# Taking the products of no use out of the first steps of a one-core attention and FFN kernel

## The chip, the cores and the metric

The kernel runs on one core of one Trainium2 chip. The metric is the device time of one execution in microseconds (us). Five engines take part, each with its own queue in order: TensorE (PE, with its weight loads as PEld), VectorE (DVE), ScalarE (ACT), GpSimd (POOL) and SyncE (SP, which issues most of the DMAs here).

## The reference

Eight batches of eight heads, 576 tokens each of head size 64. A packed query `p` of 32 rows attends over `k` and `v`, and then the 576 queries attend over the 32 packed rows, as keys and as values. The result is laid out as 4608 tokens of 512 features and goes through a two-layer FFN with a leaky activation.

```python
def sm_attn(qq, kk, vv):
    s = scale * np.matmul(qq, kk.transpose(0, 1, 3, 2))
    a = np.exp(s - np.max(s, axis=-1, keepdims=True))
    a = a / (np.sum(a, axis=-1, keepdims=True) + 1e-09)
    return np.matmul(a, vv)
p_packed = sm_attn(p, k, v)
out = sm_attn(q, p_packed, p_packed)          # -> x, 4608 x 512
h = x @ w_in                                  # 512 x 2048, float64
g = np.maximum(h, 0.0) + alpha * np.minimum(h, 0.0)
y = g @ w_out                                 # 2048 x 512, float64
```

The two weights come in as float64, and the kernel turns them into float32 by operations on their bits.

## The kernel before, in words

Heads lie in four pairs, and an FFN block is a block of 128 of the 2048 inner features. The kernel never forms x: it multiplies the packed values of a batch into `w_in` (`packed_w`, tile `pw`) and then the attention weights into that (`first`, tile `ps_h`). So an FFN block of half a batch (a "tile" k, 288 tokens) is `first(k, f)`, an activation on ACT (L783, `neg`) and one on DVE (L797, `g`), and `second(k, f)`, which adds into the four banks `acc`. In the first blocks of batch 0 these products are in plain float32 (L770 for `first`, L892 for `second`); later they are in three float32r products each (L776 to L778, and L895 to L897 or L828).

**The first steps.** Before the blocks begin, the prologue `go("...")` walks through a string, one letter for each step: `a` and `b` take one step of the attention of batch 0 and of batch 1; `i` and `o` load a piece of `w_in` or `w_out`, and `I`, `O`, `A` convert one; `0` multiplies packed values into a piece of `w_in`; `n` loads alpha. The steps of batch 0 on TensorE are in this order: the scores of `p` with `k` (L376 into `acc` from `praw`), transposes of the softmax (L653, one row of heads after the other), the products with `v` (L670), a transpose of the packed values (L513), the scores of `q` with them (L376 into `acc` from `p`), and the product into `w_in` (L376 into `ps_m` from `w`). Then the loop over blocks begins: the first piece of `pieces` is "aabb", so the scores of batch 1 (L376 into `ps_m` from `xraw`) come among the first L770 and L892.

**The products of no use.** The letters `u`, `v`, `w`, `x` call `keep_busy`, which multiplies an identity by itself into a bank that nothing reads. `v` and `w` begin with one product (L280) that reads a result of DVE (the row maxima `m0`, the row sums `z0`), so that the rest (L284) start no earlier than that.

```python
    def keep_busy(n, behind_value):
        spare = ps_h.tile([P, 512], F32, name="spare", tag="h")
        with ExitStack() as behind:
            behind.enter_context(tc.issue_after(last_mm[0].ins))
            if behind_value is not None:
                nc.tensor.matmul(
                    spare[:, : behind_value.shape[-1]], ident, behind_value, start=True, stop=True
                )
            for _ in range(n):
                last_mm[:] = [nc.tensor.matmul(spare[:, :P], ident, ident, start=True, stop=True)]
    BUSY = {"u": 7, "v": 4, "w": 4, "x": 3, "y": 3, "z": 2}
    BEHIND = {"v": "m0", "w": "z0", "z": "m1"}
```

`last_mm` is read by `keep_busy` alone. The bank `spare` has the tag `h`, of which there are two; the tiles `ps_h` of the blocks and one tile of transposes (`ps_j`) use the same two.

**What sets the order.** Each engine works off its own queue in the order that was written when the program was built. The program is built with `schedule_with_timeline_sim=True`: a planner chooses among instructions by their place in the code and by a timeline that it reckons, except where `issue_after` fixes an instruction behind another one on its engine. From place 41 of the loop on, and around the joints before that, TensorE's order is fixed by `last_pe`.

Of the kernel before, what the change touches and what calls it, by code (L numbers as in the profile page):

```python
# [27 lines left out]
def pack_attention_ffn_kernel(  # L28
# [153 lines left out]
    def load(out, in_):  # L182

        with ExitStack() as behind:
            if queue:
                behind.enter_context(tc.issue_after(queue[-1].ins))
            ins = nc.sync.dma_start(out=out, in_=in_)  # L187
        if written:
            queue[:] = [ins]
# [84 lines left out]
# [11 lines that stand above are left out]
# [414 lines left out]
    def packed_w(b, j, parts=(None,), tag=None):  # L699

        banks = [bank(tag) for _ in range(2)]
        for part_ in parts:
            to = slice(0, 512) if part_ is None else slice(part_ * 256, part_ * 256 + 256)
            for pr, r, rs, cs in heads():
                w = wi_t[j, pr] if part_ is None else w0[part_][:, pr]
                in_turn(b, banks[r][cs, to], p2[b][rs, cs], w[rs, :])
        to = slice(0, 512) if len(parts) == 2 or parts[0] is None else to
        if in_f32(b, 4 * j):
            if j % 2 == 0 and parts[0] in (None, 0):
                two_pw[:] = [pwp.tile([P, 2, 2, 512], F32, name="pw", tag="pw")]  # L710
            here = two_pw[0][:, j % 2]
        elif (b, j) == (B - 1, NJ - 1):
            here = vin.tile([P, 2, 2, 512], F32R, name="pw", tag="vraw", bufs=1)
        else:
            here = pwp.tile([P, 2, 2, 512], F32R, name="pw", tag="pw")
        times = 2.0 if half_in(j) else 1.0
        for r in range(2):
            ps = banks[r][:, to]
            if in_f32(b, 4 * j):
                a = nc.scalar.activation(out=here[:, r, to], in_=ps, func=AF.Copy, scale=times)  # L720
                anchor(b, a)
                if not first_pw and r:
                    first_pw.append(a)
            else:
                hi, lo = here[:, 0, r, to], here[:, 1, r, to]
                nc.scalar.activation(out=hi, in_=ps, func=AF.Copy, scale=times)  # L726
                nc.vector.scalar_tensor_tensor(
                    out=lo, in0=ps, scalar=times, in1=fv(hi), op0=ALU.mult, op1=ALU.subtract
                )
        for n in range(to.start // P, to.stop // P):  # L730
            cs = slice(n * P, n * P + P)
            pw[b, 4 * j + n] = here[:, :, cs] if in_f32(b, 4 * j) else here[:, :, :, cs]
# [218 lines left out]
    def go(what):  # L951


        for ch in what:
            if ch in BUSY:
                keep_busy(BUSY[ch], values[BEHIND[ch]] if ch in BEHIND else None)
            elif ch == "n":
                load(al, alpha)
                nc.gpsimd.tensor_scalar(
                    out=nal, in0=al, scalar1=-1.0, scalar2=1.0, op0=ALU.mult, op1=ALU.add  # L960
                )
            elif ch in "ab":
                next(a0 if ch == "a" else a1, None)
            elif ch in counts:
                n = counts[ch]
                counts[ch] += 1
                if ch == "0":
                    if n < 2:
                        packed_w(0, 0, (n,))
                    else:  # L970
                        packed_w(0, n - 1)
                elif ch == "1":
                    packed_w(1, n, (None,) if n else (0, 1))
                else:
                    with ExitStack() as behind:
                        for ins in tail.values() if ch != "A" else []:
                            behind.enter_context(tc.issue_after(ins.ins))
                        {
                            "i": w_in_load, "I": w_in_convert, "o": w_out_load,
                            "O": w_out_convert, "S": w_out_late_split, "H": late_a, "A": w_out_begin,  # L980
                        }[ch](n)

    go("ainaaauoiaaaIaboaiiaa0abooavbxawaOI")
    tail.clear()
    written.clear()

# [134 lines left out]
```

## Time and profile before

| what | value |
|---|---|
| median of 3 runs | 714.98 us (714.53 to 716.31) |
| the profiled execution's own time | 716.52 us |
| its span in the trace | 714.7 us |
| PE busy | 700.0 us, 98% of the span |
| DVE busy | 474.6 us, 66% |
| ACT busy | 358.2 us, 50% |
| mean granted TensorE clock | 0.993 |

The span runs from the first to the last instruction in the trace; 1.8 us of the execution's own time lie outside it. The granted clock is the share of TensorE's full speed that the throttle let through; 1.00 stands for 2.4 GHz and 0.50 for 1.2 GHz. Busy times of PE are modelled at their ends, so that the busy spans of two products in a row overlap by the tail of the first. A float32 product shows as two records.

### The profile page before, as it was taken

To read this page: it belongs to the slowest core of one execution; us is meant where nothing else is said; L and a number is where in the kernel's file an instruction comes from. 1 tells how busy PE (TensorE), PEld (TensorE's weight loads), DVE (VectorE), ACT (ScalarE), POOL (GpSimd) and SP (SyncE) were. 2 spreads that over 40 slices of the span, in tenths; PEclk is the share of its full clock that TensorE was granted. 3 is DMA by queue.
4 is the path that set the end of the run, shared out by engine and by line. 5 is a ranking of instruction groups with operands and counts; after the bars stand their busy time and mean duration, and the time that the engine had idled before them with its cause. 6 is when DMAs were issued, how large, how long until landed. Compare 5 with 4: busy or idle time off the path is not lost.

```text
span 714.7 us, 14609 instructions
## 1 busy us (share of the span) xinstructions
PE 700.0 (98%) x5604; PEld 600.7 (84%) x5604; DVE 474.6 (66%) x1067; ACT 358.2 (50%) x846; POOL 32.8 (5%) x128
## 2 busy tenths in 40 slices
PE   6999999999999999999999999999999999999997
PEld 3666998999998888888878888888887888798897
DVE  3899897974696559656783567846694446964443
ACT  3787688854355544545453454545352333533232
POOL 1000200002001100001000010001000000000000
PEclk9799999999999999999999999999999999999999
DMA  8996464332544413442314523325214103010100
GB/s 262 382 335 243 148 218 168 118 104 80 157 154 152 129 39 126 148 150 78 126 28 136 145 77 126 118 75 148 81 76 148 51 25 95 24 30 1 30 16 30
DMA packets 76740, 85.36 MB, mean 119 GB/s; under 512 B 34944, under 2 KB 56960, under 8 KB 76672
## 3 DMA queue, kind: packets, MB, share of 16 engines
q1 hardware_dynamic: 76448, 84.25, 36.6%
q8 instruction: 44, 0.72, 0.4%
q14 instruction: 24, 0.20, 0.1%
q10 hardware_dynamic: 224, 0.20, 0.1%
HBM read 70.79 MB, written 13.63 MB: 118 GB/s over the span
## 4 chain that ended last, share of the span: by engine, by line
PE 91%; DVE 4%; ACT 2%; DMA 1%; SPq 1%; issue 0%; ACTq 0%; DVEq 0%
PE acc L828 40%; PE ps_h L776 9%; PE ps_h L778 9%; PE ps_h L777 9%; PE acc L895 5%; PE acc L896 5%; PE acc L897 5%; PE ps_m L376 4%; PE ps_j L376 3%; PE acc L892 2%; PE acc L376 2%; DMA vtwo<-in_v 1%; SPq L187 1%; PE ps_h L770 1%; PE acc L928 0%
## 5 line engine op out<-in xcount | busy, mean ns | idle before, releaser
L828 PE MATMUL acc<-wo,gh 128*128 128x512 f32 x704 | 200.1, 398 | 0.0
L783 ACT ACTIVATE neg<-ps_h 128x256 f32<-128x256 f32 (+2 forms) x256 | 105.0, 411 | 161.4 <-PE ps_h L778 153.9
L797 DVE SCALAR_TENSOR_TENSOR neg<-neg,nal,ps_h 128x256 f32<-128x256 f32 (+1 forms) x248 | 119.7, 484 | 76.1 <-ACT neg L783 75.6
L807 ACT CAST gh<-neg 128x256 fp32r<-128x256 f32 (+1 forms) x248 | 101.8, 411 | 113.5 <-DVE neg L797 112.3
L776 PE MATMUL ps_h<-a_h,pw 128*128 128x256 f32 (+2 forms) x496 | 146.4, 295 | 0.4 <-DVE neg L797 0.4
L778 PE MATMUL ps_h<-a_h,pw 128*128 128x256 f32 (+2 forms) x496 | 146.6, 296 | 0.0
L777 PE MATMUL ps_h<-a_l,pw 128*128 128x256 f32 (+2 forms) x496 | 146.5, 295 | 0.0
L808 DVE TENSOR_TENSOR gl<-neg,gh 128x256 fp32r<-128x256 f32 (+1 forms) x248 | 104.7, 426 | 61.6 <-ACT gh L807 59.8
L828 PEld LDWEIGHTS acc<-wo,gh 128*128 128x128 f32 x704 | 126.7, 195 | 21.9 <-issue 4.2
L828 PE MATMUL acc<-wo,gl 128*128 128x512 f32 x352 | 115.5, 394 | 0.0
L776 PEld LDWEIGHTS ps_h<-a_h,pw 128*128 128x128 f32 x496 | 93.4, 188 | 7.4 <-DVE neg L797 1.1
L777 PEld LDWEIGHTS ps_h<-a_l,pw 128*128 128x128 f32 x496 | 93.4, 188 | 7.2
L778 PEld LDWEIGHTS ps_h<-a_h,pw 128*128 128x128 f32 x496 | 93.5, 189 | 0.1
L896 PE MATMUL acc<-gh,wo 128*128 128x288 f32 (+1 forms) x280 | 79.7, 293 | 0.5 <-DVE wo L235 0.5
L828 PEld LDWEIGHTS acc<-wo,gl 128*128 128x128 f32 x352 | 68.6, 195 | 13.5
L895 PE MATMUL acc<-gh,wo 128*128 128x288 f32 (+1 forms) x280 | 79.8, 296 | 0.0
L897 PE MATMUL acc<-gl,wo 128*128 128x288 f32 (+1 forms) x280 | 69.3, 293 | 0.0
L895 PEld LDWEIGHTS acc<-gh,wo 128*128 128x128 f32 x280 | 52.6, 189 | 4.5 <-ACT pw L726 3.4
L896 PEld LDWEIGHTS acc<-gh,wo 128*128 128x128 f32 x280 | 52.8, 189 | 1.2 <-DVE wo L235 0.7
L790 DVE SCALAR_TENSOR_TENSOR rest<-neg,nal,ps_h 128x64 f32<-128x64 f32 x96 | 26.7, 278 | 39.9 <-ACT neg L783 39.9
L897 PEld LDWEIGHTS acc<-gl,wo 128*128 128x128 f32 x280 | 48.5, 188 | 0.2 <-DVE gl L808 0.2
L828 PE MATMUL acc<-wo,rparts 128*128 128x512 f32 x144 | 35.3, 397 | 0.0
(157 smaller groups left out, 696.4 us busy)
## 6 DMA issues: line engine op xcount, KB each, us to landing
w<-w_whole SPq DMA_DIRECT2D x48, 512.0 KB, 5.7
wraw<-in_w_in SPq DMA_DIRECT2D x8, 1024.0 KB, 10.2
wraw<-in_w_out SPq DMA_DIRECT2D x8, 1024.0 KB, 6.8
xraw<-in_kT SPq DMA_DIRECT2D x28, 288.0 KB, 4.0
xraw<-in_qT SPq DMA_DIRECT2D x28, 288.0 KB, 4.4
vraw<-in_v SPq DMA_DIRECT2D x96, 64.0 KB, 2.1
outT<-out SPq DMA_DIRECT2D x44, 128.0 KB, 2.2
w_whole<-w SPq DMA_DIRECT2D x6, 512.0 KB, 7.5
```

The costliest lines, as they stand in the source:

```text
L376: mm = nc.tensor.matmul(out, lhs, rhs, start=start, stop=stop)
L776: nc.tensor.matmul(x, w[:, 0, i], a_h[:, i], start=(i == 0), stop=False)
L777: nc.tensor.matmul(x, w[:, 0, i], a_l[:, i], start=False, stop=False)
L778: mm = nc.tensor.matmul(x, w[:, 1, i], a_h[:, i], start=False, stop=(i == 1))
L783: marks[:] = [mm, nc.scalar.activation(out=neg, in_=x, func=AF.Relu, scale=-1.0)]
L797: nc.vector.scalar_tensor_tensor(out=g, in0=neg, scalar=nal[:, f : f + 1], in1=x, op0=ALU.mult, op1=ALU.add)
L807: late[:] = [nc.scalar.copy(out=gh, in_=g)]
L808: nc.vector.tensor_tensor(out=gl, in0=g, in1=fv(gh), op=ALU.subtract)
L828: mm = nc.tensor.matmul(ps, g, wo_t[f][:, part_], start=(f == 0 and i == 0), stop=(f == NF - 1 and i == 2))
L895: nc.tensor.matmul(ps, wo_t[f][:, 0, os_], gh, start=begin, stop=False)
L896: nc.tensor.matmul(ps, wo_t[f][:, 1, os_], gh, start=False, stop=False)
L897: mm = nc.tensor.matmul(ps, wo_t[f][:, 0, os_], gl, start=False, stop=end)
```

## The change

Four letters leave the prologue's string: `u`, `v`, `x` and `w`. With them go 7, 1 + 4, 3 and 1 + 4 products, 20 in all, and four uses of a bank with the tag `h`. No other letter changes its place among the rest.

```diff
-    go("ainaaauoiaaaIaboaiiaa0abooavbxawaOI")
+    go("ainaaaoiaaaIaboaiiaa0abooabaaOI")
```

## Rows read from the trace of the kernel before

**Rows 1.** The page: busy time by engine, and the chain's shares by engine.

```profile
PE 700.0 (98%) x5604; PEld 600.7 (84%) x5604; DVE 474.6 (66%) x1067; ACT 358.2 (50%) x846; POOL 32.8 (5%) x128
...
PE 91%; DVE 4%; ACT 2%; DMA 1%; SPq 1%; issue 0%; ACTq 0%; DVEq 0%
```

**Rows 2.** Busy time by stretch (us, instructions), then clock, DMA share, GB/s.

```profile
15.30:25.50 10.20, 8.73 (x137) 6.05 (x138) 7.51 (x13) 3.45 (x8) 0.00 (x0) 0.50 0.98 344
...
27.30:41.20 13.90, 12.29 (x86) 7.16 (x86) 13.46 (x24) 11.92 (x20) 0.00 (x0) 1.00 0.99 342
```

**Rows 3.** The same view in half microseconds, where the clock changes.

```profile
15.00:15.50 0.50, 0.00 (x0) 0.00 (x0) 0.47 (x2) 0.00 (x0) 0.00 (x0) 0.81 1.06 283
...
25.50:26.00 0.50, 0.50 (x6) 0.50 (x5) 0.47 (x2) 0.50 (x1) 0.00 (x0) 0.95 1.07 398
```

**Rows 4.** The tile of the products of no use: durations in ns, first and last start.

```profile
L284 PE MATMUL spare<-ident x36: 274/275/562, 9.4 to 27.0; 128*128 128x128 f32 x36
```

**Rows 5.** The chain that ended last: start, length, what.

```profile
5.65 9.85 DMA vtwo<-in_v
...
41.15 2.21 PE acc L892 x8
43.35 1.94 PE ps_h L770 x8
```

**Rows 6.** Timeline of PE, 11.5 to 30 us: start, length, records, idle before.

```profile
13.07 0.86 PE L653 MATMUL ps_j<-ident,s_t 128*128 128x128 f32 x5
...
15.54 1.28 PE L670 MATMUL ps_m<-vtwo,aT 128*32 128x64 f32 x36 [1.38 <-DMA vtwo<-in_v]
...
19.82 2.17 PE L376 MATMUL acc<-xtwo,p 64*32 64x288 f32 x32 [0.35 <-ACT p L515]
21.74 1.11 PE L376 MATMUL ps_m<-w,p 64*32 64x256 f32 x16
22.84 0.61 PE L280 MATMUL spare<-m,ident 128*128 128x18 f32 x2
...
27.34 1.21 PE L770 MATMUL ps_h<-a_f,pw 128*128 128x288 f32 x4
28.48 1.75 PE L376 MATMUL ps_m<-xraw,praw 64*32 64x288 f32 x16
```

**Rows 7.** PEld in the timeline of all engines: the last weights of those scores.

```profile
29.56 0.14 PEld L376 LDWEIGHTS ps_m<-xraw,praw 64*32 64x32 f32 x4 [0.60 <-DMA xraw<-in_kT]
```

**Rows 8.** Timeline of PE, 27 to 42 us.

```profile
30.16 1.24 PE L770 MATMUL ps_h<-a_f,pw 128*128 128x288 f32 x4
31.33 0.72 PE L376 MATMUL ps_m<-xraw,praw 64*32 64x288 f32 x16
31.98 4.25 PE L892 MATMUL acc<-g,wo_whole 128*128 128x288 f32 x16
36.52 0.67 PE L376 MATMUL ps_m<-w,p 64*32 64x256 f32 x16 [0.29 <-DVE w L144]
```

**Rows 9.** Timeline of ACT, 21 to 42 us.

```profile
29.78 0.43 ACT L783 ACTIVATE neg<-ps_h 128x288 f32<-128x288 f32 x1
...
31.44 0.41 ACT L783 ACTIVATE neg<-ps_h 128x288 f32<-128x288 f32 x1 [0.47 <-PE ps_h L770]
...
36.08 0.71 ACT L552 ACTIVATE t<-t 128x576 f32<-128x576 f32 x1
37.26 0.66 ACT L720 ACTIVATE pw<-ps_m 128x256 f32<-128x256 f32 x2 [0.46 <-PE ps_m L376]
38.45 0.78 ACT L628 ACTIVATE s_t<-s_t,nmx 128x576 f32<-128x576 f32 x1 [0.54 <-DVE nmx L627]
```

**Rows 10.** Timeline of DVE, 21 to 42.5 us.

```profile
26.41 0.78 DVE L569 STREAM_TRANSPOSE a_f<-t 128x576 f32<-128x576 f32 x1
...
33.45 0.51 DVE L797 SCALAR_TENSOR_TENSOR g<-neg,nal,ps_h 128x288 f32<-128x288 f32 x1
...
37.54 0.75 DVE L554 TENSOR_REDUCE z<-t 128x18 f32<-128x576 f32 x1
```

## The prediction

> **What bounds the kernel now.** I read the page first. TensorE is busy for 98% of the span and the chain that ended last is 91% TensorE [rows 1], so a microsecond that TensorE loses for good is a microsecond of the result, and one that it loses while it would have waited anyway is not. That is a mean over the whole kernel, and the change is in the first 28 us. So I read the busy time by stretch next, and there the picture is another. In 15.3 to 25.5 us TensorE runs at a granted clock of 0.50, which is 1.2 GHz. In 27.3 to 41.2 us, behind the removed products, VectorE is busy for 13.46 of 13.9 us, and TensorE, at full clock, for 12.29 [rows 2]. So VectorE sets the pace where the change could be felt, and TensorE has some room. The chain names three stages: up to 15.5 us a DMA of V, then short steps of TensorE and ScalarE, then VectorE until TensorE takes the chain over at 41.15 us with L892 [rows 5]. From there a delay of TensorE goes to the end in full.
>
> The clock is the second thing to see. It falls inside 15.0 to 15.5 us (mean 0.81), after a stretch in which TensorE sat idle for 1.38 us until V landed [rows 3, 6]. It rises inside 25.5 to 26.0 us (mean 0.95, so near 25.55) [rows 3], and what TensorE did ahead of that was the unbroken run of products of no use that begins at 22.84 us [rows 6].
>
> **What is removed, step by step.** Twenty float32 products, two records each: 36 records of L284, first at 9.4 and last at 27.0 us, 275 ns at the median [rows 4], and four of L280. They lie in two places: `u` (7 products, so 14 records, from 9.4 us on) and `v`, `x`, `w` together (the other 22, and the four of L280) from 22.84 us to 27.3 us, where the last record starts at 27.0 and takes some 0.27 [rows 4, 6].
>
> *Work saved: nothing on the path.* What follows `u` on TensorE, the transposes, waits for the softmax's exponentials on ScalarE, and the whole of it for V, whose landing at 15.5 us ends a wait of 1.38 us [rows 5, 6]. What follows `v`, `x`, `w` is the first L770 at 27.34 us [rows 6]. Its operand `a_f` comes from a VectorE transpose that is over at 26.41 + 0.78 = 27.19 [rows 10], so without the products it could start at most 0.15 us earlier, and its reader on ScalarE (L783) starts at 29.78 us behind other work, while L770 is over at 27.34 + 1.21 = 28.55 [rows 6, 9]. I take 0. The bounds are a gain of 0.15 and 0.
>
> *The bank.* Each use took one of the two `h` banks in turn, written and read by TensorE alone. Nothing on ScalarE or VectorE waited for it. I take 0. Were the first L770 held by it, that would again be the 0.15.
>
> *The clock without `u`.* The fall could come before 15.3 us, since TensorE then does less ahead of it. Bounded from above, both sets of transposes double: 0.86 us more for the second [rows 6] and as much again for the first, like in form, 1.72 us against the wait of 1.38, so 0.34 us late at most. From below 0. An interval of 0.86 for five records holds waits that don't double, so I take 0. The products with V that follow run at half clock already.
>
> *The clock without `v`, `x`, `w`.* This is the term that matters. The product into `w_in` ends at 21.74 + 1.11 = 22.85 us [rows 6]; then TensorE has nothing until 27.3. So the rise at 25.55 is lost, and L770 begins at half clock. The question is when the rise comes (call it R) and what it costs by then. No row shows R; I price four places.
>
> Prices: eight records of L770 or L892 take 1.94 us at full clock [rows 5], so four take 0.97, and at half clock 1.94. A batch-1 score set (16 records) takes 0.72 with its tail at full clock [rows 8] and 2.17 / 2 = 1.08 at half [rows 6].
>
> - R at 27.3: no cost, 0.
> - R near 33. First L770: 27.3 to 29.25, tail to 29.5; L783 at 29.78 [rows 9] feels nothing. First scores: today they last 1.75 us, since their last weights wait for a DMA until 29.56 [rows 6, 7], so half clock adds only some 0.5: over at 30.8. Second L770: starts a tail of 0.24 ahead of that, 30.55, over at 32.5 + 0.24 = 32.74 instead of 30.16 + 1.24 = 31.40 [rows 8]. So its L783 on ScalarE comes 1.3 us late (32.74 for 31.44 [rows 9]). The VectorE step that reads it (L797) starts at 33.45 [rows 10], and 32.74 + 0.41 = 33.15 is in time. Behind it on ScalarE everything is queued up to 1.3 later. L552 then ends at 36.08 + 0.71 + 1.3 = 38.09, and VectorE wants that at 37.54 [rows 9, 10]: 0.55 us late. The next two waits of ScalarE, 0.46 and 0.54 us [rows 9], use up most of the rest. TensorE itself: scores to 33.1, L892 for 3.88 to 37.0, so the product at 36.52 is 0.5 late [rows 8], and L720 behind it no later than ScalarE is already. Cost at 41.15: 0.55 us.
> - R near 36. The scores end at 33.5, L892 does 2.5 us at half clock (1.25 of its 3.88), then 2.63 at full: 38.6 for 36.52, so 2.1 late, L720 too. ScalarE's wait of 0.54 at 38.45 absorbs a part [rows 9]. Cost 1.6 us.
> - R near 39. L892 does 5.5 us at half clock, 2.75 of 3.88, then 1.13 more: 40.1, so 3.6 late, less 0.54: 3.1 us. That needs half clock through nearly the whole of an unbroken set of L892.
>
> Which? In the trace, the rise came 2.7 us after the run of spare products began (22.84 to 25.55) [rows 3, 6]. That is one event and no rule. A like lag from 27.3 gives 30.0 and a cost of 0; from 30.55, where TensorE's queue no longer waits for a DMA, 33.3 and some 0.5; from the first L892 at 33.5, 36.2 and 1.6. I take the middle one: 0.5 us.
>
> **The sum.** 0 + 0 + 0 + 0.5 = 0.5 us. The profiled execution took 716.52 us for a span of 714.7, with 1.8 us outside the span; by its own time the changed kernel comes to 717.0. Against the median of the runs, 714.98, that is 715.5, and 0.07% is no difference that can be told: about 0.3% (2.1 us, so 712.8 to 717.1) is what a measurement of this kernel can tell from no change.
>
> **A rule that speaks against the change.** The row: TensorE's clock fell after idle time and rose only behind the spare products [rows 3, 6]. The Trainium skill, "TensorE: Matmul & The Clock Gate", section "Why this matters for your kernels", says to leave no long idle gaps between bursts of matmuls, because they drop the engine to half clock. The fall at 15.3 us agrees with it. By that rule alone the change makes the kernel slower, as the first rival does; by the rows VectorE covers most of it.
>
> **The rivals.**
>
> *1. Slower: half clock until 39 us.* Place: the two sets of L892, planned for 31.98 to 36.23 [rows 8]. For it: the rise of before had a dense run of full 128 x 128 products, and what now stands there is mixed with score sets on 64 x 32 tiles, which at 19.82 to 22.0 us did not raise the clock [rows 2, 6]. Against it: from 27.3 us on TensorE has always something to do. It decides from R of about 37, where the lateness reaches 2.6 and the cost 2.1 us; at 39 it gives 714.98 + 3.1 = 718.1. Later still, each further microsecond of half clock adds half a microsecond.
>
> *2. Slower: another order.* The queue order comes from a planner's timeline, and 20 products fewer change what TensorE has free there. If the batch-1 scores came ahead of the first L770 on TensorE, L770 would wait for the DMA of 29.56 [rows 7] and end near 32.5 at half clock; L783 at 29.78 [rows 9] would come 2.7 us late, and VectorE with it. Price 2 to 3 us: about 717.5. Against it: only `keep_busy` reads `last_mm`, and no other step is fixed behind the products removed.
>
> *3. Faster: another order.* The same doubt with luck. What could be won in 27.3 to 41.2 us is VectorE's idle time, 13.9 - 13.46 = 0.44 us [rows 2]. Together with the 0.15 that is 714.4, still no difference. More needs a different order behind 41 us, too.
>
> *4. The change is felt at once, as less work for TensorE.* By the page (98% busy) 20 products would be worth their busy time, 14 records of 0.275 at most (3.9 us) and 22.84 to 27.3 (4.5) [rows 4, 6]: 8.4 us, 706.6. Against it: both lie in TensorE's waiting time, as shown above.
>
> **How the numbers follow.** Forecast (R up to about 37, no gain): 0.70. Rival 1 beyond 2.1 us: 0.14. Rival 2: 0.10. Rival 3 with more than 2.1 us won: 0.05. Rival 4: 0.01. So faster 0.06, same 0.70, slower 0.24. The time of the likeliest is 715.5. Its own range is 714.4 (0.59 us won) to 716.6 (R near 36). The range for 8 in 10 reaches up into the slower rivals to 717.7, and down to 714.0, which is the lower end and the scatter of 0.45 us that the runs show below their median.
>
> **What the profile would show.** Right: no L280 and L284; TensorE idle from 22.85 to 27.3 us; clock at 0.50 without a break from 15.3 us or earlier to 30 to 36 us; V still landing near 15.5; the first L770 near 27.3 but twice as long; VectorE still busy without a gap in 29 to 41 us; L892 of the second block at 41.2 to 42.6 us. Wrong: a clock of 0.50 beyond 37 us, VectorE waiting for ScalarE's L783 or L552 by more than 2 us, the batch-1 scores ahead of the first L770, or a different order of VectorE's conversions. It would also be wrong if TensorE's waits behind 41 us changed, since I take the rest of the span as it is.

## The result: 0.8% slower, and the profile after

The changed kernel took 720.35 us (median of 4, 719.42 to 721.36) against 714.75 of the kernel before (median of 4 on the same chip): a ratio of 1.0078 [1.0064, 1.0092], or 5.6 us more. The forecast was 715.5 us with a range up to 717.7, so the measured time lies above it. The profiled execution took 721.36 us for a span of 719.6, with 1.8 us outside of it as before. Ratios in what follows leave out the few executions far above the rest (of the kernel before 762 and 972 us, of e13 1139 and 1742 us), and medians keep them.

The page after: busy time by engine, TensorE's granted clock in 40 slices of some 18 us, and the chain's shares by engine.

```profile
PE 695.2 (97%) x5564; PEld 596.2 (83%) x5564; DVE 474.7 (66%) x1067; ACT 357.4 (50%) x846; POOL 32.8 (5%) x128
...
PEclk8699999999999999999999999999999999999999
...
PE 89%; DVE 4%; ACT 4%; DMA 1%; issue 1%; SPq 1%; ACTq 0%; DVEq 0%
```

TensorE is busy 4.8 us less and the kernel is 5.6 us slower [rows 1]: that work was no part of what sets the end. ScalarE's share of the chain has doubled to 4%, which is the first hint.

Busy time by stretch after, to be held against [rows 2, 3] (us, then PE, PEld, DVE, ACT and POOL with their instructions, clock, DMA share, GB/s).

```profile
14.05:27.40 13.35, 6.08 (x125) 3.41 (x125) 9.33 (x16) 5.77 (x10) 0.00 (x0) 0.50 1.00 355
27.40:41.00 13.60, 10.95 (x72) 5.57 (x72) 13.06 (x22) 9.27 (x16) 0.00 (x0) 0.86 1.00 330
...
31.00:31.50 0.50, 0.50 (x2) 0.43 (x3) 0.50 (x2) 0.50 (x2) 0.00 (x0) 0.88 1.03 410
...
41.40:44.80 3.40, 3.40 (x9) 2.27 (x8) 0.53 (x3) 0.41 (x1) 0.00 (x0) 0.50 1.10 410
```

The clock is 0.50 from 14.05 us without a break to 31.1 (a mean of 0.88 over 31.0 to 31.5 puts the rise near 31.12), and VectorE stays busy, 13.06 of 13.6 us: both as forecast. What was not forecast is the last row, a second fall, 41.4 to 44.8 us.

TensorE's timeline after, beside [rows 6, 8] (start, length, what, and in brackets the idle time before and what ended it).

```profile
20.33 1.11 PE L376 MATMUL ps_m<-w,p 64*32 64x256 f32 x16
21.18 1.22 PE L376 MATMUL acc<-xtwo,p 64*32 64x288 f32 x16
27.48 2.26 PE L770 MATMUL ps_h<-a_f,pw 128*128 128x288 f32 x4 [5.08 <-DVE a_f L569]
...
32.11 0.69 PE L376 MATMUL ps_m<-xraw,praw 64*32 64x288 f32 x8
33.00 2.21 PE L892 MATMUL acc<-g,wo_whole 128*128 128x288 f32 x8 [0.20 <-DVE g L797]
35.14 0.69 PE L376 MATMUL ps_m<-xraw,praw 64*32 64x288 f32 x8
...
38.03 0.66 PE L376 MATMUL ps_m<-w,p 64*32 64x256 f32 x16
41.05 3.90 PE L770 MATMUL ps_h<-a_f,pw 128*128 128x288 f32 x8 [2.36 <-ACT pw L720]
44.78 0.71 PE L653 MATMUL ps_m<-ident,s_t 128*128 128x128 f32 x5
45.33 1.14 PE L770 MATMUL ps_h<-a_f,pw 128*128 128x288 f32 x4
46.30 2.10 PE L892 MATMUL acc<-g,wo_whole 128*128 128x288 f32 x8
```

TensorE before, at the same two places:

```profile
37.69 2.21 PE L770 MATMUL ps_h<-a_f,pw 128*128 128x288 f32 x8 [0.51 <-ACT pw L720]
...
41.15 2.21 PE L892 MATMUL acc<-g,wo_whole 128*128 128x288 f32 x8 [0.70 <-DVE g L797]
```

Two things are to be seen. The first is a new wait: 2.36 us ahead of the L770 of 41.05, which waited 0.51 before (at 37.69), and those eight records then take 3.90 us instead of 2.21, nearly all of it at half clock. The second is that the queue itself is another. The product into `w_in` now stands between the two halves of the scores of `q` (20.33 ahead of 21.18; before, behind both [rows 6]); the batch-1 scores are split around L892, 8 records on each side (before, 16 in one set at 31.33 [rows 8]); and at 45.33 an L770 stands ahead of the L892 that took the chain over before [rows 5].

ScalarE's timeline after, at the place of [rows 9].

```profile
39.86 0.77 ACT L628 ACTIVATE s_t<-s_t,nmx 128x576 f32<-128x576 f32 x1 [1.93 <-DVE nmx L627]
...
40.63 0.64 ACT L720 ACTIVATE pw<-ps_m 128x256 f32<-128x256 f32 x2
44.07 0.41 ACT L783 ACTIVATE neg<-ps_h 128x288 f32<-128x288 f32 x1 [2.80 <-PE ps_h L770]
```

This is where the wait comes from. Before, L720 (the second piece of `pw`, read by that L770) stood ahead of L628, the exponentials of batch 1 [rows 9]. Now it stands behind. The product it takes from the bank is over at 38.69, but ScalarE sits at L628, which needs row maxima from VectorE, until 39.86, and L720 starts at 40.63. A queue in order makes L720 wait for an operand that is not its own.

The two queues side by side (`-` before, `+` after; ScalarE, from 33.5 us on in the trace after; tile numbers left out):

```diff
 L176 ACTIVATE rest<-wraw
-L599 COPY s_t<-ps_m x2
-L177 ACTIVATE rest<-wraw
 L552 ACTIVATE t<-t
-L720 ACTIVATE pw<-ps_m x2
+L599 COPY s_t<-ps_m
+L177 ACTIVATE rest<-wraw
+L599 COPY s_t<-ps_m
 L628 ACTIVATE s_t,den<-s_t,nmx
+L720 ACTIVATE pw<-ps_m x2
 L783 ACTIVATE neg<-ps_h x2
```

With the products of no use left aside, the queues differ at 52 places of TensorE, 15 of ScalarE, 40 of VectorE and 9 of SyncE, all in the first 70 us, and nowhere else. VectorE's are of the same kind; its timeline after, at the place of [rows 10]:

```profile
26.56 0.78 DVE L569 STREAM_TRANSPOSE a_f<-t 128x576 f32<-128x576 f32 x1
...
30.17 1.22 DVE L178 CUSTOM_DVE_ANT_0 wo_whole<-wo_whole,rest 128x2048 uint16<-128x2048 uint16 x1
31.30 1.22 DVE L140 SCALAR_TENSOR_TENSOR w<-wraw,w 128x1024 uint32<-128x1024 uint32 x1
32.44 0.51 DVE L797 SCALAR_TENSOR_TENSOR g<-neg,nal,ps_h 128x288 f32<-128x288 f32 x1
```

The first `g` (L797) now stands behind L140; before, it ran at 31.23 and L140 after it.

TensorE's waits after, from 20 us to the end (waited for: us in total, times, longest):

```profile
PE ps_h L770 <- DVE a_f L569: 5.1, 1, 5.1
PE ps_h L770 <- ACT pw L720: 2.4, 1, 2.4
PE ps_m L670 <- DVE pw L727: 1.4, 1, 1.4
```

The first stands where the products of no use were. The second is the one above. The third, at 64.7 us, is new as well: the products with V of batch 1 wait for a piece of `pw` that VectorE makes.

**Where the time went.** V's landing differs a little between executions, so I count from the first product behind that landing (L670). Starts in us behind it, from the timelines; e1, e3 and e16 are experiments told below, and all five profiles run the products with V at half clock:

| TensorE starts | before | after | e1 | e3 | e16 |
|---|---|---|---|---|---|
| (L670 itself, from the span's start) | 15.54 | 15.08 | 13.95 | 14.61 | 15.16 |
| first L770 | 11.80 | 12.40 | 11.80 | 12.41 | 11.80 |
| product into `w_in` ahead of L720 | 20.98 | 22.95 | 21.85 | 22.94 | 22.47 |
| L770 that reads L720's piece | 22.15 | 25.97 | 23.04 | 24.08 | 23.61 |
| L653 | 24.20 | 29.70 | 25.08 | 26.13 | 25.66 |
| L670 of batch 1 | 44.98 | 49.65 | 45.20 | 46.31 | 46.71 |
| end of the span | 699.16 | 704.52 | 699.35 | 700.49 | 700.84 |

The changed kernel is 0.60 us late at the first L770, 1.97 at the product, 3.82 behind the wait for L720, 5.50 behind the eight records at half clock. Some is given back up to 64 us (before has a wait of 0.70 for `g` at 41.15 that is gone), the wait at L670 costs again, and 5.36 us remain at the end. Of the 0.7 us that come behind the L670 of batch 1, 0.36 is one idle stretch of TensorE that no view puts to another engine; the rest I did not find.

### The profile page after: what moved, and what is told of

Read it like the earlier page. It is cut to its first block, busy times and chain, and to the rows that moved or that the text cites. A ratio compares the mean times of both kernels' runs of the same rounds, so it can differ in the third digit from the quotient of the medians.

```text
span 719.6 us, 14528 instructions
## 1 busy us (share of the span) xinstructions
PE 695.2 (97%) x5564; PEld 596.2 (83%) x5564; DVE 474.7 (66%) x1067; ACT 357.4 (50%) x846; POOL 32.8 (5%) x128
## 4 chain that ended last, share of the span: by engine, by line
PE 89%; DVE 4%; ACT 4%; DMA 1%; issue 1%; SPq 1%; ACTq 0%; DVEq 0%
PE acc L828 39%; PE ps_h L776 9%; PE ps_h L778 9%; PE ps_h L777 9%; PE acc L895 5%; PE acc L896 5%; PE acc L897 4%; PE ps_m L376 3%; PE ps_j L376 3%; PE acc L376 1%; DMA vtwo<-in_v 1%; PE ps_h L770 1%; SPq L187 1%; ACT rest L177 1%; ACT rest L176 0%
## 5 line engine op out<-in xcount | busy, mean ns | idle before, releaser
L783 ACT ACTIVATE neg<-ps_h 128x256 f32<-128x256 f32 (+2 forms) x256 | 105.2, 412 | 166.1 <-PE ps_h L778 155.1
L797 DVE SCALAR_TENSOR_TENSOR neg<-neg,nal,ps_h 128x256 f32<-128x256 f32 (+1 forms) x248 | 119.6, 483 | 77.0 <-ACT neg L783 76.6
L778 PE MATMUL ps_h<-a_h,pw 128*128 128x256 f32 (+2 forms) x496 | 146.6, 296 | 0.0
L777 PE MATMUL ps_h<-a_l,pw 128*128 128x256 f32 (+2 forms) x496 | 146.5, 295 | 0.0
L828 PEld LDWEIGHTS acc<-wo,gh 128*128 128x128 f32 x704 | 126.7, 195 | 21.9 <-issue 4.2
L777 PEld LDWEIGHTS ps_h<-a_l,pw 128*128 128x128 f32 x496 | 93.4, 188 | 7.2
L778 PEld LDWEIGHTS ps_h<-a_h,pw 128*128 128x128 f32 x496 | 93.5, 189 | 0.1
L895 PE MATMUL acc<-gh,wo 128*128 128x288 f32 (+1 forms) x280 | 79.8, 296 | 0.0
L895 PEld LDWEIGHTS acc<-gh,wo 128*128 128x128 f32 x280 | 52.6, 189 | 4.5 <-ACT pw L726 3.4
```

The lines of the kernel that those rows point to most:

```text
L777: nc.tensor.matmul(x, w[:, 0, i], a_l[:, i], start=False, stop=False)
L778: mm = nc.tensor.matmul(x, w[:, 1, i], a_h[:, i], start=False, stop=(i == 1))
L783: marks[:] = [mm, nc.scalar.activation(out=neg, in_=x, func=AF.Relu, scale=-1.0)]
L797: nc.vector.scalar_tensor_tensor(out=g, in0=neg, scalar=nal[:, f : f + 1], in1=x, op0=ALU.mult, op1=ALU.add)
L828: mm = nc.tensor.matmul(ps, g, wo_t[f][:, part_], start=(f == 0 and i == 0), stop=(f == NF - 1 and i == 2))
L895: nc.tensor.matmul(ps, wo_t[f][:, 0, os_], gh, start=begin, stop=False)
```

## The experiments

Two theories. **The order**: the 5.6 us come from the new queues, which the planner wrote because 20 instructions were gone, whatever the products did for TensorE. **The clock** (the rival): they come from the half clock without the products. To part them I fixed the queues by hand: at the end of the program each instruction is put behind the one that shall precede it on its engine, for the first 185 of TensorE, 65 of ScalarE, 85 of VectorE and 60 DMA issues, which takes in every place that differs. The lists are read off the kernel before (`old`) or after (`new`); products of no use are in no list.

```diff
+    queued = {"PE": old["PE"], "Activation": old["ACT"], "DVE": old["DVE"], "SP": old["SP"]}
...
+    for e, places in queued.items():
+        for one, then in zip(places, places[1:]):
+            tc.add_manual_dep(
+                real[e][then], real[e][one].name,
+                mybir.DependencyInfo(mybir.DependencyClass.NoSync, mybir.DependencyReason.DATA),
+                reason="queued",
+            )
```

No kernel leaves out or changes a part of the reference's computation; some have more or fewer products of no use. Lines of kernels so edited stand some lower: L720 is L723 or L721 there, L628 is L631, L770 is L773, L775, L777 or L778, L670 is L673, L727 is L730. Times are medians; ratios are to the kernel before in the same rounds on the same chip. Kernels of different rounds ran on different chips, where before's own median lies between 714.75 and 715.17 us, so a difference of two medians across them is uncertain by some 0.4 us at least.

### The order against the products: e1, e2

e1 has no products of no use, and all four queues `old`, by the edit above.

> The changed kernel (no products of no use), with the first 185 TensorE, 65 ScalarE, 85 VectorE and 60 DMA instructions fixed in the queue order of the kernel before. Order theory (the planner's new queue order cost the 5.6 us, above all ScalarE's L720 now standing behind L628): 714.8 to 716.4 us, the 0 to 1.6 us that half clock alone was priced at, and no wait of TensorE over 1 us between 28 and 60 us. Clock theory (TensorE at half clock until 31 us costs it, whatever the order): 718 us or more.

Measured: 715.91 us beside 715.17 of before, 1.0006 [0.9997, 1.0016]. The clock in its profile is 0.50 from 13.72 to 30.79 us, as long as in the changed kernel (17.07 us each):

```profile
13.50:14.00 0.50, 0.05 (x4) 0.05 (x7) 0.47 (x2) 0.43 (x2) 0.00 (x0) 0.72 1.04 297
14.00:30.50 16.50, 10.78 (x148) 5.88 (x149) 14.21 (x22) 8.73 (x14) 0.00 (x0) 0.50 1.04 384
30.50:31.00 0.50, 0.50 (x2) 0.05 (x1) 0.50 (x2) 0.00 (x0) 0.00 (x0) 0.71 1.00 401
```

Some half a microsecond, not clear of none, is all that the products are worth where the order is kept. TensorE's timeline of e1:

```profile
25.75 2.26 PE L773 MATMUL ps_h<-a_f,pw 128*128 128x288 f32 x4 [4.49 <-DVE a_f L572]
...
29.09 2.06 PE L773 MATMUL ps_h<-a_f,pw 128*128 128x288 f32 x4
...
31.73 4.15 PE L895 MATMUL acc<-g,wo_whole 128*128 128x288 f32 x16
35.80 0.66 PE L379 MATMUL ps_m<-w,p 64*32 64x256 f32 x16
36.99 2.21 PE L773 MATMUL ps_h<-a_f,pw 128*128 128x288 f32 x8 [0.53 <-ACT pw L723]
39.03 0.71 PE L656 MATMUL ps_m<-ident,s_t 128*128 128x128 f32 x5
39.81 2.21 PE L895 MATMUL acc<-g,wo_whole 128*128 128x288 f32 x8
```

The first L770 takes 2.26 us instead of 1.21 [rows 6], and TensorE is 0.88 us late at L653. The L892 behind it (39.81, here L895) no longer has before's wait of 0.70 for `g` [rows 5], and starts 25.86 us behind V's landing where before had 41.15 - 15.54 = 25.61: 0.25 us are left.

e2 is the reverse, all products of no use and all four queues `new`.

```diff
-    go("ainaaaoiaaaIaboaiiaa0abooabaaOI")
+    go("ainaaauoiaaaIaboaiiaa0abooavbxawaOI")
+    queued = {"PE": new["PE"], "Activation": new["ACT"], "DVE": new["DVE"], "SP": new["SP"]}
```

> The kernel before with all its products of no use, with the same stretch of the queues fixed in the order of the changed kernel. Order theory: TensorE's wait for L720 stays (2.4 us near 38 to 41 us) although the clock is back by 26 us, so 717 to 719.5 us. Clock theory: 714.8 to 715.5 us, as before.

Measured: 719.67 us, 1.0064 [1.0051, 1.0077], just above the 719.5 that the order theory gave and far from the 715.5 of the clock theory. Its profile has full clock up to 40.45 us, mean 0.998, and its median is within 0.7 us of the changed kernel's. TensorE waits 2.35 us for L723 (L720) here too. Its clock by stretch, and that wait in its timeline:

```profile
15.00:40.00 25.00, 18.43 (x223) 10.45 (x223) 22.09 (x36) 14.96 (x24) 0.00 (x0) 1.00 1.00 357
...
40.57 3.82 PE L773 MATMUL ps_h<-a_f,pw 128*128 128x288 f32 x8 [2.35 <-ACT pw L723]
```

The two by two:

| | products in | products out |
|---|---|---|
| order of before | 715.2 | 715.9 |
| order of after | 719.7 | 720.35 |

So the order is the cause, some 4.5 to 5 us with either (by medians or by ratios), and the clock theory is left with 0.4 to 1.0. Fixing queues by hand costs nothing that shows: e1 above and e8, e12 and e17 below are level with the kernel before.

### The one place on ScalarE: e3, e5, e6, e18

e3 is the changed kernel with L628 put behind L720 on ScalarE, and nothing else fixed.

```diff
+                second_exp.append(a)
...
+                if second_exp and parts == (1,):
+                    tc.add_manual_dep(
+                        second_exp[0].ins, a.ins.name,
+                        mybir.DependencyInfo(mybir.DependencyClass.NoSync, mybir.DependencyReason.DATA),
+                        reason="pw first",
+                    )
```

> The changed kernel with one edge in ScalarE's queue: the first L628 behind L720, so that pw no longer waits behind the exponential of batch 1. Order theory in its narrow form (this one place): L720 at 38.8 instead of 40.6 us, TensorE's wait 2.36 down to about 0.7, no second fall of the clock at 41.4 us (1.7 us more): about 717 us (716.3 to 717.9). Order theory in its wide form (many places): 718 to 719.5. Clock theory: unchanged, 719.4 to 721.4.

Measured: 716.98 us, 1.0024 [1.0015, 1.0033]. One place gives back 3.4 us by the medians, 3.9 by the ratios. ScalarE's timeline in its profile, L721 being L720:

```profile
38.26 0.66 ACT L721 ACTIVATE pw<-ps_m 128x256 f32<-128x256 f32 x2 [0.81 <-PE ps_m L376]
39.38 0.78 ACT L628 ACTIVATE s_t<-s_t,nmx 128x576 f32<-128x576 f32 x1 [0.47 <-DVE nmx L627]
```

And TensorE's, the L770 that reads it and the L653 behind:

```profile
38.69 2.21 PE L777 MATMUL ps_h<-a_f,pw 128*128 128x288 f32 x8 [0.48 <-ACT pw L721]
40.74 0.71 PE L654 MATMUL ps_m<-ident,s_t 128*128 128x128 f32 x5
```

The wait is 0.48 us instead of 2.36, the eight records take 2.21 instead of 3.90, and the clock does not fall a second time. L628 loses nothing by it: it starts at 39.38, when its row maxima are there.

e5 is the reverse: the kernel before with its queues fixed, but L628 ahead of L720.

```diff
 ScalarE, all else as before
+L628
 L720
 L720
-L628
```

> The kernel before, products of no use and all, with its own queue order fixed on every engine but for one place: ScalarE's first L628 (the exponential of batch 1) stands ahead of the two L720 of the second piece of pw, as in the changed kernel. Theory that this one place carries most of the loss: L720 starts near 39.3 instead of 37.3 us, TensorE waits over 2 us for it, and the clock may fall behind that wait: +2 to +4 us, 717 to 719. Theory that the loss is spread over many places: within 1 us of the kernel before, 714.7 to 716.2.

Measured: 717.60 us (715.64 to 720.10) beside 715.09, 1.0033 [1.0017, 1.0048]: 2.4 us from one place, with all the products of no use in. TensorE's timeline of e5:

```profile
38.44 2.85 PE L773 MATMUL ps_h<-a_f,pw 128*128 128x288 f32 x8 [3.00 <-ACT pw L723]
41.08 1.27 PE L656 MATMUL ps_m<-ident,s_t 128*128 128x128 f32 x5
42.15 2.67 PE L895 MATMUL acc<-g,wo_whole 128*128 128x288 f32 x8
```

The wait is there, 3.00 us, and behind it the clock falls (0.50 from 39.86 to 43.28), so it is not the missing products that let it fall at this place.

e6 is the changed kernel, queues `new`, with two places of ScalarE put back: L720 ahead of L628, and L177 ahead of L659.

```diff
 ScalarE, all else as after
+L720, L720
 L628
-L720, L720
...
+L177
 L659, L659
-L177
```

> The changed kernel with its own queue order fixed on every engine but for two places on ScalarE: L720 ahead of L628, as in e3_pw_ahead, and L177 (the rest for the second half of w_out) ahead of the two L659 copies, so that VectorE's L178 no longer waits 0.7 us for it and its L727, which TensorE waits 1.1 to 1.4 us for near 61 us, comes sooner. If these two places are all that is lost beside the clock: 715.5 to 716.3. If the rest lies elsewhere (the split scores, TensorE's other order): as e3_pw_ahead, 716.7 to 717.2.

Measured: 717.05 us, 1.0024 [1.0013, 1.0035], the same as e3. The second place is worth nothing.

e18 is e3's place with SyncE's queue `old` as well.

```diff
+    queued = {"PE": new["PE"], "Activation": pw_ahead(new["ACT"]), "DVE": new["DVE"], "SP": old["SP"]}
```

> The changed kernel in its own order but for ScalarE's L720 ahead of L628 and the DMA queue, which is in the old order. If these two account for the loss beside the clock: 715.4 to 716.3. If not: 716.6 to 717.4, as e3_pw_ahead.

Measured: 716.57 us, 1.0022 [1.0011, 1.0033]. The DMA order adds nothing to e3.

### The second fall of the clock: e4, e7

e4 puts the letter `v` back into the changed kernel, 5 products behind the row maxima.

```diff
-    go("ainaaaoiaaaIaboaiiaa0abooabaaOI")
+    go("ainaaaoiaaaIaboaiiaa0abooavbaaOI")
```

> The changed kernel with the letter v put back alone: five products of no use behind the row maxima, and the planner leaves every other instruction in the changed kernel's order. Order theory: 719 to 721.4 us, but without what the second fall of the clock costs if that goes away. Clock theory: the clock comes back a few us sooner than 31 us, so 716 to 718 us.

Measured: 721.09 us, 1.0081 [1.0069, 1.0093]. The other instructions stand just as in the changed kernel. The clock rose at 23.49 us, fell again at 26.90, rose at 30.32 and had the fall of 40.56 to 43.97. Three microseconds of full clock ahead of 27 us bought nothing: TensorE waits there in any case, and the clock had fallen again before the first L770 (27.34), which takes 2.26 us as in the changed kernel.

e7 is the changed kernel, queues `new`, with 8 products of no use behind the product into `w_in`, where TensorE waits for L720.

```diff
+        if (b, j, parts) == (0, 0, (1,)):
+            keep_busy(8, None)
```

> The changed kernel in its own queue order, with eight products of no use put into TensorE's wait for L720 near 38.7 to 41 us, so that TensorE is busy there. If the second fall of the clock at 41.4 us costs what the eight L770 behind it lose (3.90 us for 2.21), the runs lie at 718.7 to 719.6 with no run above 720.5. If that loss is hidden behind ScalarE or VectorE: 720.0 to 721.4 as the changed kernel.

TensorE's timeline of e7, the added products and the L770 behind them:

```profile
38.64 2.05 PE L286 MATMUL spare<-ident 128*128 128x128 f32 x16
40.88 2.21 PE L775 MATMUL ps_h<-a_f,pw 128*128 128x288 f32 x8 [0.18 <-ACT pw L723]
```

Measured: 720.34 us (718.08 to 721.36), 1.0063 [1.0044, 1.0082]. In the profile the clock does not fall at this place and the eight records take 2.21 us, 1.69 less; counted from V's landing the end of the span comes 0.84 us sooner (703.68 for 704.52). The median shows no gain, and two of the six executions (718.08, 719.22) lie below what was expected for none, so neither expectation was met. Executions fall into two groups by their mean clock (last section); group for group e7 lies 0.6 to 0.8 us under the changed kernel, which fits the 0.84, but with six executions against four on another chip that is a hint. What the second fall costs by itself is not shown.

### Engine by engine: e9, e10, e11, e16, e17

All five have no products of no use. e9 has only ScalarE's queue `old`, e10 only VectorE's, e11 both of them (TensorE and SyncE `new`), e16 all but TensorE's, e17 all but SyncE's.

```diff
+    queued = {"PE": new["PE"], "Activation": old["ACT"], "DVE": new["DVE"], "SP": new["SP"]}
```

> The changed kernel with ScalarE's queue alone fixed in the order of the kernel before; TensorE, VectorE and DMA queues stay in the changed kernel's order. If ScalarE's order is nearly all of the loss: 715.7 to 716.4, near e1_old_order_no_spares. If only its L720 matters and the rest is VectorE's or TensorE's order: 716.6 to 717.3, as e3_pw_ahead.

Measured: 718.70 us, 1.0049 [1.0034, 1.0063], above both ranges.

```diff
+    queued = {"PE": new["PE"], "Activation": new["ACT"], "DVE": old["DVE"], "SP": new["SP"]}
```

> The changed kernel with VectorE's queue alone fixed in the order of the kernel before. ScalarE's L720 still stands behind L628, so by the theory of that place 718 to 720; what it is below the changed kernel's 720.35 is VectorE's own part (its L797 behind L170, L136, L178, L140). Below 717 would refute that L720's place is the larger part.

Measured: 718.07 us, 1.0042 [1.0028, 1.0056].

```diff
+    queued = {"PE": new["PE"], "Activation": old["ACT"], "DVE": old["DVE"], "SP": new["SP"]}
```

> The changed kernel with ScalarE's and VectorE's queues both in the order of the kernel before; TensorE's and the DMA queue in the changed kernel's order (the product into w_in between the two score sets, the second batch-1 scores split around an L892). If TensorE's own order costs nothing: 715.4 to 716.4, as e1_old_order_no_spares. If it costs the 1 us that e3_pw_ahead and e6_two_swaps leave: 716.6 or more.

Measured: 717.60 us, 1.0026 [1.0015, 1.0036]. ScalarE's whole old queue (e9) is worth 1.7 us and the one place of it in e3 3.4: the parts don't add up. In e9 the wait for L720 is down to 0.5 us, but TensorE waits 0.6 us for `g` ahead of an L770 and 0.5 us for ScalarE's exponentials ahead of an L653, waits that neither the kernel before nor the changed one has at these places.

```diff
+    queued = {"PE": new["PE"], "Activation": old["ACT"], "DVE": old["DVE"], "SP": old["SP"]}
```

> As e11_act_dve_old, with the DMA queue in the old order as well, so that TensorE's order alone is the changed kernel's. If the DMA order (the store of the converted w_in moved ahead of the loads of q and of the next weights) is what e11, e13 and e14 lose: 715.4 to 716.2. If TensorE's order is: 716.6 to 717.6, as those.

Measured: 717.11 us beside 715.08, 1.0025 [1.0015, 1.0035], against 1.0006 of e1: TensorE's new order alone costs some 1.4 us. Its timeline of TensorE shows a wait for that:

```profile
61.87 1.47 PE L673 MATMUL ps_m<-vraw,aT 128*32 128x64 f32 x80 [1.56 <-DVE pw L730]
```

It is the third wait of the changed kernel. The product that this piece of `pw` comes from is not late: counted as in the table above its one set starts 41.40 us behind V's landing (56.56), and the last of its two sets in e1 41.37 (55.32). VectorE is: it does L730 behind its conversions and comes to it at 45.97 (61.13) for 44.46 (58.41) in e1, 1.51 us late. ScalarE hands on TensorE's order in two places, in e16's timelines of VectorE and ScalarE (L557 is L554 of before, L555 is L552, L662 is L659, L656 is L653):

```profile
37.94 0.75 DVE L557 TENSOR_REDUCE z<-t 128x18 f32<-128x576 f32 x1 [0.75 <-ACT t L555]
...
49.66 0.75 ACT L662 COPY aT<-ps_m 128x384 f32<-128x384 f32 x2 [0.88 <-PE ps_m L656]
```

At the first VectorE falls 0.53 us behind e1: ScalarE's copies wait for the split batch-1 scores, and its L552 comes behind them. At the second the lateness grows to some 1.5: the transposes L653 now stand behind an L770, and what ScalarE does behind their copies reaches VectorE later. In the table, e16 is 1.73 us late at L670, and e1 0.22.

```diff
+    queued = {"PE": old["PE"], "Activation": old["ACT"], "DVE": old["DVE"], "SP": new["SP"]}
```

> No products of no use, all of ScalarE, VectorE and TensorE in the old order, and the DMA queue alone in the changed kernel's. If the DMA order carries it: 716.4 to 717.2. If TensorE's order does: 715.4 to 716.1, as e1_old_order_no_spares.

Measured: 715.02 us beside 715.08, 1.0003 [0.9992, 1.0014], a little under the lower range. The DMA order costs nothing that shows. Beside e17, of the same rounds, e16 is 2.1 us slower.

### Which places of TensorE: e13, e14, e15

TensorE's list differs in an early part (the product between the scores of `q`, the batch-1 scores around L892) and a late part (L770 ahead of L892 and of L653, the product in one set). e13 is e11 with the late part put back, e14 with the early part, e15 is e3's place with the late part.

```diff
+    queued = {"PE": late_old(new["PE"]), "Activation": old["ACT"], "DVE": old["DVE"], "SP": new["SP"]}
```

> As e11_act_dve_old (ScalarE's and VectorE's queues in the order of the kernel before), and on TensorE the three late places back in the old order as well: L892 ahead of the second pair of L770, the second batch-1 transposes (L653) ahead of L770, and the product into w_in split around L892. The three early places (the product into w_in between the score sets, the scores split around L892) stay in the changed kernel's order. In e11 ScalarE's L659 copies wait 0.84 us for those L653, and all of VectorE runs 0.9 us later from there. If the late places are what e11 loses: 715.6 to 716.4, as e1_old_order_no_spares. If the early places are: 717 to 717.8, as e11.

Measured: 716.80 us, 1.0023 [1.0013, 1.0033], between the two ranges.

```diff
+    queued = {"PE": early_old(new["PE"]), "Activation": old["ACT"], "DVE": old["DVE"], "SP": new["SP"]}
```

> The other half: as e11_act_dve_old, with TensorE's three early places back in the old order and the three late ones in the changed kernel's. If the late places are what e11 loses: 716.8 to 717.6. If the early places are: 715.6 to 716.4.

Measured: 716.67 us, 1.0021 [1.0012, 1.0030], between the two ranges as well.

```diff
+    queued = {"PE": late_old(new["PE"]), "Activation": pw_ahead(new["ACT"]), "DVE": new["DVE"], "SP": new["SP"]}
```

> The changed kernel in its own order but for ScalarE's L720 ahead of L628 (as e3_pw_ahead) and TensorE's three late places, which are put back in the old order. If these two account for the loss beside the clock: 715.6 to 716.4. If VectorE's order keeps a part of it: 716.6 to 717.3, as e3.

Measured: 718.26 us, 1.0040 [1.0025, 1.0055], above both ranges and no better than e3, though the wait at L670 is down from 1.4 us to 0.4 in its profile. Neither half of TensorE's order is the cause alone: each leaves some 0.002 where e11 has 0.0026 and e1 0.0006. The profiles part the two places of e16: with the early part old (e14) VectorE no longer waits for L552, and TensorE still waits 1.54 us for L730; with the late part old (e13) VectorE waits 0.64 us for L552, and TensorE not for L730. The times don't follow: e13's median is still 1.7 us above before. Its profiled execution was its fastest (715.38 us), so what holds the others was not seen. Some of these differences may be a matter of which executions were caught: of the two groups of the last section the faster has 1 of 10 in e13 and 3 of 12 in e1. Which place of TensorE costs how much stays open.

### Products of no use in the wait for V: e8, e12

Both are the kernel before, queues `old`, with products of no use added where TensorE waits for V: 6 into a bank of the tag `h` (e8), or 4 into a bank `ps_m` (e12).

```diff
+        if b == 0:
+            last_mm[:] = [tr]
+            keep_busy(6, None)
```

> The kernel before in its own queue order, with six more products of no use in TensorE's wait for V near 14 to 15.5 us, so that the clock has no reason to fall there. Runs of the kernel before with a mean granted clock of 1.00 took 714.1 to 714.9 us, those with 0.993 took 716.0 to 716.7. If that clock is the cause, all runs of this kernel lie at 714.0 to 714.9, about 0.6 us below the median of the kernel before. If the two go together by chance, or the added products come late and hold up the products with V: 715 to 716.5.

Measured: 715.35 us beside 715.09, 1.0004 [0.9994, 1.0014]. The bank came free late, the added products began at 14.26 us and held the products with V until 15.80.

```diff
+            keep_busy(4, None, True)
...
+        spare = bank() if own else ps_h.tile([P, 512], F32, name="spare", tag="h")
```

> As e8_v_wait_filled, but four more products instead of six, and in a bank ps_m that comes free sooner, so that they are over before V lands and hold up nothing. If the clock in that stretch costs time and e8 lost its gain to its late products: all runs at 714.0 to 714.9, median 714.5, under the kernel before by some 0.6 us. If the clock there costs nothing: 715.1, as the kernel before.

TensorE's timeline of e12, the four added products and those with V:

```profile
12.86 1.16 PE L286 MATMUL ps_m<-ident 128*128 128x128 f32 x8
13.95 0.30 PE L678 MATMUL ps_m<-vtwo,aT 128*32 128x64 f32 x4
14.72 0.75 PE L678 MATMUL ps_m<-vtwo,aT 128*32 128x64 f32 x36 [0.47 <-DMA vtwo<-in_v]
```

Measured: 714.47 us (713.98 to 715.67) beside 715.07, 0.9993 [0.9984, 1.0003]. The products with V take 0.75 us at full clock instead of 1.28 [rows 6]. Its median is the lowest of all versions run, and not clear of the kernel before; its executions, up to 715.67 us, do not all lie in the range expected.

## Why the prediction was wrong, point by point

- **The sum was right for what it priced.** Work saved 0, bank 0, clock 0 and 0.5: e1, which has those terms and no other, measured 0.4 us [-0.2, +1.1], which is also not clear of 0.
- **The clock without `u`: held.** The fall came at 14.05 us after and 13.72 in e1, ahead of V's landing (15.08, 13.95). Nothing there was late beyond the 0.34 of the bound.
- **The clock without `v`, `x`, `w`: held, in place and path, and in price within 0.3 us.** R was taken near 33; it was 31.12 after and 30.79 in e1, which on before's count from V's landing is 31.6 and 32.4. The steps of that case, as e1 has them behind before: second L770 late by 0.39 forecast, 0.52 measured; first L892 1.1 and 1.34; product 0.5 and 0.87; the L892 that takes the chain over 0.55 and 0.25. The path was the forecast one, ScalarE's L552 to VectorE's L554 (L555 and L557 in e1), where VectorE is late by those 0.25 us from here on; the size, 0.55, was too large:

```profile
36.20 0.75 DVE L557 TENSOR_REDUCE z<-t 128x18 f32<-128x576 f32 x1 [0.23 <-ACT t L555]
```
- **Rival 1 was wrong.** The clock rose at 31.1 us, not 39; its rise fell within the first batch-1 steps, ahead of any L892. What was said for the rival does not hold in every trace either: in e7 the clock rose near 21.9 us, while TensorE worked on score sets on 64 x 32 tiles and with no product of no use ahead of it.
- **The step that failed is the queues, which the sum put at nothing.** Its four terms price work, bank and clock, with every due time of [rows 8 to 10] read as if the queues stayed ("I take the rest of the span as it is"); so L720 was to come "no later than ScalarE is already". The runs showed that ScalarE had L628 ahead of L720 now, TensorE waited 2.36 us there for 0.51, and the whole new order cost some 4.5 to 5 us of the 5.6 (e1, e2). The 0.70 given to "R up to about 37, no gain" had no condition on the order.
- **Rival 2 named the mechanism and gave it 0.10.** Its place was wrong: the batch-1 scores did not come ahead of the first L770. Its price of 2 to 3 us is that of the place found (e5: 2.4 us), but there were more places than one. What spoke against it, that only `keep_busy` reads `last_mm`, was no evidence: that holds for fixed orders, and the rest is chosen by the planner's timeline, in which 20 products took up TensorE's time. Why the planner chose so was not tried; that its new choice holds without the products and with them is shown (e2).
- **The price of a swap could have been read from [rows 9].** L628 waits 0.54 for VectorE right behind L720. Put first, it would have held L720 until 38.45 + 0.78 = 39.23 instead of 37.26, some 2 us. The two stand next to each other, L628 due by VectorE, L720 due by TensorE, and nothing but the planner's reckoning decides which is first.
- **Rival 4 was wrong**, by the page: 4.8 us less of TensorE, and nothing gained.
- **Three of the signs named for "wrong" came**: another order of VectorE's conversions, VectorE waiting for L783 by more than 2 us (its L797 at 44.51 waits 2.87), and other waits of TensorE behind 41 us (0.70 for `g` gone, 1.42 at L670 new). The clock was up before 37 us and then at 0.50 once more from 41.4 us, which is another fall than the sign had in mind; the batch-1 scores stayed behind the first L770.

## What to carry to other kernels

Where a planner writes the queues, a removed instruction is an edit to every queue near it, so compare the queues ahead of any argument on work or clock, and forecast with a term for a swap: two neighbours in one queue with different releasers, priced by how long the first can wait. Fix the order by hand before taking out or adding filler, and the filler's own worth can be measured; here it was 0.4 us, with 0 inside the interval. An engine's order is good only beside the others': putting back one whole queue (1.7 us) gave less than one edge in it (3.4).

## What the hardware showed that was not expected

- **The mean granted clock differs from execution to execution of one kernel, and the time with it.** Of 23 executions of the kernel before beside e1, those with a mean granted clock of 0.998 and more took 714.1 to 715.7 us, and those of 0.992 to 0.995 took 715.4 to 716.7. Its profiled execution (0.993, 716.52 us) was one of the latter, and the fall at 15.3 us [rows 3], on which the forecast's half-clock steps rest, is not in every one: its 10.2 us at half clock [rows 2] make the 0.993, and 7 of the 23 have 1.000. e1 has the same two groups without the products, 714.1 to 714.9 at 0.992 and 715.1 to 716.9 at 0.986 to 0.989; the changed kernel has them at 719.4 and 719.6 (0.990) and at 721.2 and 721.4 (0.986). Within a group the products are worth no more than their scatter, and the order some 5 us. That the clock makes the difference between the groups is not shown: e8 has 0.997 and more in all of its executions, and they spread from 714.6 to 716.8 us.
- **V landed at different times**: the product that waits for it started at 13.95 to 15.63 us in the profiles of before, after, e1 to e3, e5, e10, e12 and e16. A start counted from the span's beginning is uncertain by that much.
- **An idle stretch of 2.36 us of TensorE was followed by 3.4 us at half clock** (after), of 3.00 by 3.4 (e5), and 0.5 us by none (e1, e3). The Trainium skill, "TensorE: Matmul & The Clock Gate", section "Why this matters for your kernels", warns of idle gaps between bursts for this reason. The trace agrees that the clock falls; the time saved by filling that gap could not be told from none (e7). The length alone does not tell: before's 1.38 us ahead of 15.54 ended with the clock falling [rows 3, 6], while at e5's 1.07 ahead of 15.10 and the changed kernel's 1.42 ahead of 64.73 it stayed at 1.00.
